# A fused attention and mixer kernel: the first channel product of the last two token groups as seven half products instead of eight

## Chip, cores and metric

The kernel runs on one core of one Trainium2 chip. The metric is the device time of one execution in microseconds (us). The engines are PE (TensorE; PEld is its weight load), DVE (VectorE), ACT (ScalarE), POOL (GpSimd) and SP (SyncE, which here only issues DMAs). Differences under about 0.5% (4.15 us here) can't be told from no change by a measurement of this kernel.

## What is computed

With 8 batches, 8 heads, 576 tokens and head size 64, and with d_model 512, 256 token-mixing and 1536 channel-mixing units:

```python
q_s = softmax(q, axis=-1);  k_s = softmax(k, axis=2)           # over features, over tokens
x   = q_s @ (k_s^T @ v)                                        # per head, put together to (8, 576, 512)
xt  = x.transpose(0, 2, 1)
u   = x + (relu(xt @ w_tok1) @ w_tok2).transpose(0, 2, 1)      # token mixing
out = u + relu(u @ w_ch1) @ w_ch2                              # channel mixing: "ch1", then "ch2"
```

## The kernel before

**Tiling.** The 8 x 576 tokens are cut into nine groups of 512 tokens. A group's u is kept transposed, channels on the partitions, as four tiles of 128 channels x 512 tokens (index n), each split into a high and a low float32r part (`uh`, `ul`). There are three such slots, which the groups take in turn (`uT`, L355). ch1 is cut into twelve row blocks f of 128 hidden channels; the weights of block f stand in `cw[f]` as four parts: 0 and 1 are ch1's high and low part, 2 and 3 ch2's.

**A step** is one (group, f). `ch1(g, f)` (L400) runs 12 matmuls of 512 columns: for each n, low weights by high tokens, high by high, high by low. ACT takes the relu into `h2h` (L410) and DVE the rounding rest into `h2l` (L411). `ch2` (L415) adds 12 more matmuls into four accumulators `ps_o`, one for each n of the output. In the main loop (L564) ch1 of a step is written ahead of ch2 of the step before it, so that the relu has a whole ch1 to finish in. After a group's last step `residual` (L427) adds `uh` and `ul` on POOL into `stg` tiles (a pool of two buffers of 128 x 1024 floats), and `out_end` (L436) adds the accumulators on DVE into these `stg` tiles and sends them out.

**Attention beside it.** The 32 units (batch, head pair) of attention and token mixing are spread over the steps up to the group before the last but one, one unit every three steps (`put`, L544; `todo`). A unit uses all engines: `softmax_k` subtracts a maximum on POOL (`k_t`, L235); `softmax_q` ends in a split of q whose rest is made on POOL (`ql`, L115); `stage_qT` turns q on DVE and copies 32 x 32 blocks back in 16 pieces (L321, eleven on DVE, five on ACT), which must wait for `ql`, since they write over its input; `stage_h1` and `stage_u` make the token mixing: the relu `hh` on ACT (L350), its rest `hl` on DVE (L351), and matmuls that take both (L379).

**What sets the order.** The program is written as above, but a scheduler of the build reorders the instructions of each engine; the order is then fixed, and each engine runs its own list strictly in turn. Loads are issued by SP in such a list too: `q_t`, `v_t`, `k_t` and `kt_t` for the units.

## Time and profile before

| | |
|---|---|
| runs | 827.21, 830.62, 830.99 us; median 830.62 |
| the profiled execution | 830.2 us, of which 828.3 us are the span of the profile |
| TensorE clock granted | 1.00 in the whole span |
| PE / PEld busy | 796.6 us (96%) / 669.5 us (81%) |
| DVE / ACT / POOL busy | 487.7 us (59%) / 331.6 us (40%) / 113.0 us (14%) |
| ch1, L407 | 1296 matmuls of 128 x 512; ch2, L419: as many |
| DMA | 63.54 MB, 77 GB/s on average |

Rows of the time line give start, duration, engine, source line, operation, out<-in, count, and in brackets the idle time ahead with what ended it. Rows of groups end in busy time, mean duration in ns and idle time. Rows of waits give total us, how often, the longest. Matmuls are pipelined: the distance of their starts is their cost, not the duration in the row (390 ns for 512 columns).

### The profile page before, as it was taken

To read this page: it belongs to the slowest core of one execution; us is meant where nothing else is said; L and a number is where in the kernel's file an instruction comes from. 1 tells how busy PE (TensorE), PEld (TensorE's weight loads), DVE (VectorE), ACT (ScalarE), POOL (GpSimd) and SP (SyncE) were. 2 spreads that over 40 slices of the span, in tenths; PEclk is the share of its full clock that TensorE was granted. 3 is DMA by queue.
4 is the path that set the end of the run, shared out by engine and by line. 5 is a ranking of instruction groups with operands and counts; after the bars stand their busy time and mean duration, and the time that the engine had idled before them with its cause. 6 is when DMAs were issued, how large, how long until landed. Compare 5 with 4: busy or idle time off the path is not lost.

```text
span 828.3 us, 11791 instructions
## 1 busy us (share of the span) xinstructions
PE 796.6 (96%) x4464; PEld 669.5 (81%) x4464; DVE 487.7 (59%) x1084; ACT 331.6 (40%) x822; POOL 113.0 (14%) x93
## 2 busy tenths in 40 slices
PE   4799999988999999999999999999999999999997
PEld 3688888777888888788888888888888888888886
DVE  6899998899775555665556554755566322112112
ACT  6876534455543344344434443344434321011110
POOL 1000000112220111311113111311131102001000
PEclk9999999999999999999999999999999999999999
DMA  9753433423212122322232211321131001001001
GB/s 297 235 160 94 146 108 102 138 76 114 90 48 92 53 63 60 100 63 63 63 113 63 63 47 36 108 63 53 42 97 47 15 1 51 1 0 51 1 1 51
DMA packets 60632, 63.54 MB, mean 77 GB/s; under 512 B 40864, under 2 KB 40992, under 8 KB 60576
## 3 DMA queue, kind: packets, MB, share of 16 engines
q1 hardware_dynamic: 55392, 53.36, 21.9%
q10 hardware_dynamic: 5184, 9.44, 3.0%
q8 instruction: 35, 0.57, 0.3%
q14 instruction: 21, 0.17, 0.1%
HBM read 53.35 MB, written 9.44 MB: 76 GB/s over the span
## 4 chain that ended last, share of the span: by engine, by line
PE 77%; DVE 11%; DMA 6%; issue 2%; ACT 2%; POOL 1%; SPq 1%; DVEq 0%; POOLq 0%; ACTq 0%
PE ps_h L407 30%; PE ps_o L419 30%; PE ps_h L379 6%; PE ps_h L335 5%; DVE q_t L321 3%; DMA out<-stg 2%; PE ps_h L275 2%; DMA q_t<-in_q 2%; PE ps_h L343 1%; PE ps_o L379 1%; DMA stg<-in_w 1%; PE ps_h L233 1%; DVE st L243 1%; POOL ql L115 1%; DMA kt_t<-in_kt 1%
## 5 line engine op out<-in xcount | busy, mean ns | idle before, releaser
L407 PE MATMUL ps_h<-uh,cw 128*128 128x512 f32 x864 | 268.3, 391 | 1.3 <-DVE cw L115 1.3
L419 PE MATMUL ps_o<-h2h,cw 128*128 128x512 f32 x864 | 250.0, 391 | 0.0
L419 PEld LDWEIGHTS ps_o<-h2h,cw 128*128 128x128 f32 x864 | 160.2, 188 | 32.6 <-ACT h2h L410 0.2
L407 PEld LDWEIGHTS ps_h<-uh,cw 128*128 128x128 f32 x864 | 159.3, 188 | 32.4 <-DVE cw L115 1.7
L411 DVE SCALAR_TENSOR_TENSOR h2l<-ps_h,h2h 128x512 fp32r<-128x512 f32 x108 | 74.3, 688 | 171.3 <-ACT h2h L410 170.2
L407 PE MATMUL ps_h<-ul,cw 128*128 128x512 f32 x432 | 168.6, 390 | 0.0
L410 ACT ACTIVATE h2h<-ps_h 128x512 fp32r<-128x512 f32 x108 | 64.6, 598 | 251.0 <-PE ps_h L407 234.6
L419 PE MATMUL ps_o<-h2l,cw 128*128 128x512 f32 x432 | 151.9, 395 | 1.0 <-DVE h2l L411 1.0
L321 DVE COPY q_t<-cv_s 32x160 f32<-32x160 f32 (+1 forms) x264 | 70.5, 267 | 63.9 <-POOL ql L115 60.6
L407 PEld LDWEIGHTS ps_h<-ul,cw 128*128 128x128 f32 x432 | 81.1, 188 | 17.4
L419 PEld LDWEIGHTS ps_o<-h2l,cw 128*128 128x128 f32 x432 | 79.6, 188 | 17.4 <-DVE h2l L411 1.4
L235 POOL TENSOR_TENSOR k_t<-k_t,mb 128x640 f32<-128x640 f32 x24 | 38.1, 1586 | 298.6 <-ACT mb L234 298.6
L115 POOL TENSOR_TENSOR ql<-q_t,qh 128x640 fp32r<-128x640 f32 x24 | 37.6, 1566 | 211.9 <-ACT qh L114 180.8
L432 POOL TENSOR_TENSOR stg<-uh,ul 128x512 f32<-128x512 f32 x28 | 35.6, 1292 | 143.5 <-DMA out<-stg 118.8
L243 DVE TENSOR_REDUCE st<-q_t 128x10 f32<-128x640 f32 x32 | 26.2, 818 | 37.6 <-DMA q_t<-in_q 37.5
L254 ACT ACTIVATE q_t<-q_t 128x640 f32<-128x640 f32 x28 | 20.7, 741 | 44.3 <-DVE q_t L253 40.8
L321 ACT COPY q_t<-cv_s 32x128 f32<-32x128 f32 (+1 forms) x120 | 36.8, 307 | 1.9 <-DVE cv_s L313 0.5
L379 PE MATMUL ps_h<-w2h,hl 128*128 128x320 f32 (+1 forms) x112 | 30.1, 302 | 4.3 <-DVE hl L351 4.1
L379 PE MATMUL ps_h<-w2h,hh 128*128 128x256 f32 (+1 forms) x112 | 32.7, 299 | 0.0
L379 PE MATMUL ps_h<-w2l,hh 128*128 128x256 f32 (+1 forms) x112 | 32.6, 296 | 0.0
L386 ACT CAST uh<-ps_h 128x320 fp32r<-128x320 f32 (+4 forms) x76 | 24.5, 339 | 14.7 <-PE ps_h L379 9.0
L387 DVE TENSOR_TENSOR ul<-ps_h,uh 128x320 fp32r<-128x320 f32 (+4 forms) x76 | 26.7, 372 | 5.3 <-ACT uh L386 4.4
(140 smaller groups left out, 1048.4 us busy)
## 6 DMA issues: line engine op xcount, KB each, us to landing
stg<-in_w SPq DMA_DIRECT2D x28, 512.0 KB, 4.1
kt_t<-in_kt SPq DMA_DIRECT2D x32, 320.0 KB, 3.5
q_t<-in_q SPq DMA_DIRECT2D x32, 320.0 KB, 3.0
v_t<-in_v SPq DMA_DIRECT2D x64, 128.0 KB, 3.1
out<-stg ACTq DMA_DIRECT2D x32, 256.0 KB, 3.2
k_t<-in_k SPq DMA_DIRECT2D x24, 320.0 KB, 3.6
v_t<-in_v SPq DMA_DIRECT2D x32, 32.0 KB, 3.2
out<-part ACTq DMA_DIRECT2D x4, 256.0 KB, 2.6
```

What stands on the lines that cost most here:

```text
L115: lo_eng.tensor_tensor(lo, src, f32(hi), op=ALU.subtract)
L235: nc.gpsimd.tensor_tensor(kx, kx, mb.unsqueeze(1).broadcast_to([P, C1, P]), op=ALU.subtract)
L243: nc.vector.tensor_reduce(st[:, 0, :], qt, axis=AX.X, op=ALU.max)
L321: eng(qx[ys, 0:n, xs], turned[xs, 0:n, ys])
L335: nc.tensor.matmul(y[:, 0:TOK], a, w, start=(i == 0), stop=(i == len(mm) - 1))
L379: nc.tensor.matmul(t[:, 0:N], a, w, start=(i == 0), stop=(i == len(mm) - 1))
L387: nc.vector.tensor_tensor(ul, src, f32(uh), op=ALU.subtract).ins,
L407: nc.tensor.matmul(t, cw[f][x][:, n, :], w, start=(i == 0), stop=(i == 3 * NJ - 1))
L410: nc.scalar.activation(hh, t, AF.Relu).ins,
L411: nc.vector.scalar_tensor_tensor(hl, t, 0.0, f32(hh), op0=ALU.max, op1=ALU.subtract).ins,
L419: nc.tensor.matmul(o, cw[f][x][:, n, :], w, start=(first and i == 0), stop=(last and i == 2))
L432: nc.gpsimd.tensor_tensor(res[n], f32(uh), f32(ul), op=ALU.add)
```

## The change

For the last two groups (but for the first two row blocks of the last group but one) two row blocks fa, fb are taken together as a pair. Their ch1 is seen as a 2 x 2 block product: two row blocks by two halves of the contraction (n = 0, 1 and n = 2, 3), times two halves of the contraction by two halves of the tokens (256 each). Eight half products of 6 matmuls with 256 columns would be what stands there now; the new `pair` makes seven, four of them with sums of weight blocks and four with sums of token blocks, and puts the results together by adds on DVE before the relu. There are eleven such pairs: five of the last group but one, six of the last.

- `weight_sums(p)` makes the four sums of the weights of pair p, splits them and writes high and low part to a buffer in memory: on POOL two adds of 128 x 512, four of 128 x 256 and one subtraction of 128 x 1024, on ACT one copy of 128 x 1024, on SP two DMAs of 512 KB in rows of 512 B. It takes two tiles of the `stg` pool. The six calls are put two to a group into the fourth, fifth and sixth group, whose other work is the attention units.
- `load_sum` brings the sums back, 256 KB for each half product in two DMAs, to five places in `cw` that are free by then; each is started when the place's last user is done, five half products ahead.
- `token_sums(g)` makes four sums of token blocks on DVE (nine operations of 128 x 512) and splits them (four copies on ACT, four subtractions on DVE).
- In `pair` each half product goes through one or two adds on DVE (128 x 256; the first is copied by ACT), and the relu and its rest are made in four pieces of 128 x 256 instead of two of 128 x 512. ch2 of the pair before is written between the half products (`between`).

```diff
+    HC = CW // 2
+    def weight_sums(p):
+        a, b = cw[2 * p], cw[2 * p + 1]
+        x = stg.tile([P, CW, 2], U32, name="stg").rearrange("p n w -> p (n w)")
+        xf, xr = x.bitcast(F32), x.bitcast(F32R)
+        for i, (hi, lo) in enumerate((a[:2], b[:2])):
+            both = xf[:, i * CW : (i + 1) * CW].rearrange("p (n m) -> p n m", n=NJ)
+            nc.gpsimd.tensor_tensor(both, f32(hi), f32(lo), op=ALU.add)
+        a11, a12, a21, a22 = (xf[:, i * HC : (i + 1) * HC] for i in range(4))
+        nc.gpsimd.tensor_tensor(a22, a21, a22, op=ALU.add)
+        nc.gpsimd.tensor_tensor(a21, a11, a21, op=ALU.subtract)
+        nc.gpsimd.tensor_tensor(a11, a22, a11, op=ALU.subtract)
+        nc.gpsimd.tensor_tensor(a12, a12, a11, op=ALU.subtract)
+        h = stg.tile([P, CW, 2], U32, name="stg").rearrange("p n w -> p (n w)").bitcast(F32R)
+        nc.scalar.copy(h, xf)
+        nc.gpsimd.tensor_tensor(xr, xf, f32(h), op=ALU.subtract)
+        for i, t in enumerate((h, xr)):
+            src = f32(t).rearrange("p (k n m) -> p k n m", k=4, n=2)
+            nc.sync.dma_start(sums[p][:, :, :, i, :], src)
...
+    def token_sums(g, place, tmp):
...
+        def cut(k, t):
+            hi, lo = place[k]
+            split(hi, lo, t, nc.vector)
...
+    def product(weights, rows):
+        t = ps_h.tile([P, 512], F32, name="ps_h")[:, 0:HC]
+        i = 0
+        for n in range(2):
+            uh, ul = (x[:, n, :] for x in rows)
+            for x, w in ((1, uh), (0, uh), (0, ul)):
+                nc.tensor.matmul(t, weights(x, n), w, start=(i == 0), stop=(i == 5))
+                i += 1
+        return t
...
+        def drain(f, t, src):
+            hh, hl = (x[:, t * HC : (t + 1) * HC] for x in hs[f])
+            nc.scalar.activation(hh, src, AF.Relu)
+            nc.vector.scalar_tensor_tensor(hl, src, 0.0, f32(hh), op0=ALU.max, op1=ALU.subtract)
...
+        nc.scalar.copy(v0, product(own(fa, 0), half(0, 0)))
+        plus(v1, own_sum(S2, tsum[g, 2]), v0)
+        between(0)
+        plus(v0, product(own(fa, 2), half(1, 0)), v0)
+        drain(0, 0, v0)
+        plus(v2, own_sum(S3, tsum[g, 3]), v1)
+        between(1)
+        t = own_sum(S1, tsum[g, 1])
+        plus(v3, t, v2)
+        plus(v1, t, v1)
+        drain(1, 1, v3)
+        plus(v2, product(own(fb, 2), tsum[g, 4]), v2)
+        drain(1, 0, v2)
+        between(2)
+        plus(v1, own_sum(S4, half(1, 1)), v1)
+        drain(0, 1, v1)
+        between(3)
...
+    for p in range(NF // 2):
+        put(n0 + NF * (p // 2 + 1) + (5, 9)[p % 2], lambda p=p: weight_sums(p))
```

**What moves on POOL.** The first place is POOL's list at the start of the fourth group, the first of the three groups that take weight sums. Before it reads as follows (`k_t` and `ql` belong to the units, `stg<-uh,ul` is `residual` of the group that begins).

```order
L235 TENSOR_TENSOR k_t<-k_t,mb 128x640
L432 TENSOR_TENSOR stg<-uh_101,ul_105 128x512 x2
L115 TENSOR_TENSOR ql<-q_t,qh 128x640
L432 TENSOR_TENSOR stg<-uh_101,ul_105 128x512 x2
L235 TENSOR_TENSOR k_t<-k_t,mb 128x640
L115 TENSOR_TENSOR ql<-q_t,qh 128x640
```

Now the list begins at the same `k_t` so (L443 to L451 are `weight_sums`; the other lines stand one further down, `residual` is L570):

```order
L236 TENSOR_TENSOR k_t<-k_t,mb 128x640
L443 TENSOR_TENSOR stg<-cw_117 128x512 x2
L116 TENSOR_TENSOR ql<-q_t,qh 128x640
L445 TENSOR_TENSOR stg<-stg 128x256
L446 TENSOR_TENSOR stg<-stg 128x256
L447 TENSOR_TENSOR stg<-stg 128x256
L448 TENSOR_TENSOR stg<-stg 128x256
L451 TENSOR_TENSOR stg<-stg 128x1024
L443 TENSOR_TENSOR stg<-cw_117 128x512 x2
```

After the four small adds of the second sums, the same list goes on to the next unit:

```order
L448 TENSOR_TENSOR stg<-stg 128x256
L236 TENSOR_TENSOR k_t<-k_t,mb 128x640
L451 TENSOR_TENSOR stg<-stg 128x1024
L570 TENSOR_TENSOR stg<-uh_101,ul_105 128x512 x2
L116 TENSOR_TENSOR ql<-q_t,qh 128x640
L570 TENSOR_TENSOR stg<-uh_101,ul_105 128x512 x2
```

So the first sums stand where `residual` stood, around the first unit's `ql`, and `residual` has moved one unit later, around the second `ql`, behind the second sums. The same change stands at the start of the fifth and sixth group. The order of PE's list is the same as before up to the first pair.

**What moves on ACT** at the same place: the copy of the first sums (L450) has come in between the relu `hh` of the unit and the relu of a step.

```order
L351 ACTIVATE hh<-ps_h 128x256
L450 CAST stg<-stg 128x1024
L411 ACTIVATE h2h_108<-ps_h 128x512
L115 CAST qth<-q_t 128x576
L387 CAST uh_100<-ps_h 128x256
```

Without the row of L450 these are the rows of before. What POOL subtracts in L451 waits for it.

**What moves on DVE** where the pairs begin, at the end of the last unit and the change from the seventh to the eighth group. Before:

```order
L387 TENSOR_TENSOR ul_104<-ps_h,uh_100 128x64
L387 TENSOR_TENSOR ul_106<-ps_h,uh_102 128x320
L387 TENSOR_TENSOR ul_106<-ps_h,uh_102 128x192
L443 TENSOR_TENSOR stg<-ps_o,stg 128x512 x4
L411 SCALAR_TENSOR_TENSOR h2l_112<-ps_h,h2h_108 128x512
L411 SCALAR_TENSOR_TENSOR h2l_113<-ps_h,h2h_109 128x512
```

Now, from the fifth token sum behind the last `ul` on (L466 and L116 are `token_sums`, `tmp` its intermediate sums, L581 is `out_end`):

```order
L466 TENSOR_TENSOR tmp_6670<-tmp_6670,ul_106 128x512
L581 TENSOR_TENSOR stg<-ps_o,stg 128x512
L466 TENSOR_TENSOR tmp_6672<-tmp_6672,ul_104 128x512
L581 TENSOR_TENSOR stg<-ps_o,stg 128x512
L466 TENSOR_TENSOR tmp_6673<-tmp_6673,ul_104 128x512
L581 TENSOR_TENSOR stg<-ps_o,stg 128x512
L466 TENSOR_TENSOR tmp_6670<-tmp_6670,ul_106 128x512
L581 TENSOR_TENSOR stg<-ps_o,stg 128x512
L412 SCALAR_TENSOR_TENSOR h2l_112<-ps_h,h2h_108 128x512
L116 TENSOR_TENSOR ul_105<-tmp_6672,uh_101 128x512
L116 TENSOR_TENSOR ul_105<-tmp_6673,uh_101 128x512
L412 SCALAR_TENSOR_TENSOR h2l_113<-ps_h,h2h_109 128x512
```

The token sums of both groups have been drawn forward between the adds of `out_end` and the rests of the two single steps; those of the last group go on into the first pair, where ten more operations of 128 x 512 stand between the pair's own eleven of 128 x 256.

## The prediction, made before the changed kernel was run

> **What bounds the kernel now.** I read the page's busy shares and its chain first, then the waits of PE from the third group on, then the time lines of the stretches that the change touches.

> ```profile
> PE 796.6 (96%) x4464; PEld 669.5 (81%) x4464; DVE 487.7 (59%) x1084; ACT 331.6 (40%) x822; POOL 113.0 (14%) x93
> ...
> PE 77%; DVE 11%; DMA 6%; issue 2%; ACT 2%; POOL 1%; SPq 1%; DVEq 0%; POOLq 0%; ACTq 0%
> ```
> ```profile
> PE ps_h L379 <- DVE hl L351: 2.7, 3, 1.7
> ```

> PE is the bound, and behind 250 us it is almost never late: three waits with 2.7 us in all, each where a unit's matmuls L379 need `hl`. So matmuls saved are time saved, and any new wait of PE is time lost. The busy shares say nothing of the second; the stretches do.

> **Part 1, the matmuls.** The cost of a matmul is the distance of starts. One stretch of PE's time line has both widths:

> ```profile
> 336.33 0.62 PE L407 MATMUL ps_h<-uh,cw 128*128 128x512 f32 x2
> ...
> 339.05 0.28 PE L335 MATMUL ps_h<-w1h,qh 128*128 128x256 f32 x1
> ...
> 340.72 0.64 PE L419 MATMUL ps_o<-h2h,cw 128*128 128x512 f32 x2
> ...
> ```

> From 336.33 to 339.05 run 12 matmuls of 512 columns: 2.72 us, 0.2267 each. From 339.05 to 340.72 run the 14 of L335 with 256 columns, each with its own weights: 1.67 us, 0.1193 each, 5% above the half. A pair had 24 x 0.2267 = 5.44 us of ch1 and gets 42 x 0.1193 = 5.01; it saves 0.43 us instead of the 0.68 of an exact eighth. Eleven pairs: **-4.7 us**. That is the whole gain; ch2 is unchanged.

> **Part 2, the weight sums in groups four to six.** They are off PE, but their POOL work stands ahead of things that PE waits for. Start of the fourth group, POOL, DVE and ACT:

> ```profile
> 335.70 1.57 POOL L235 TENSOR_TENSOR k_t<-k_t,mb 128x640 f32<-128x640 f32 x1 [15.28 <-ACT mb L234]
> 343.17 2.53 POOL L432 TENSOR_TENSOR stg<-uh,ul 128x512 f32<-128x512 f32 x2 [5.89 <-DMA out<-stg]
> 345.66 1.56 POOL L115 TENSOR_TENSOR ql<-q_t,qh 128x640 fp32r<-128x640 f32 x1
> 347.18 2.54 POOL L432 TENSOR_TENSOR stg<-uh,ul 128x512 f32<-128x512 f32 x2
> 359.65 1.57 POOL L235 TENSOR_TENSOR k_t<-k_t,mb 128x640 f32<-128x640 f32 x1 [9.93 <-ACT mb L234]
> 365.81 1.57 POOL L115 TENSOR_TENSOR ql<-q_t,qh 128x640 fp32r<-128x640 f32 x1 [4.60 <-ACT qh L114]
> ```
> ```profile
> 347.26 4.79 DVE L321 COPY q_t<-cv_s 32x160 f32<-32x160 f32 x11 [4.57 <-POOL ql L115]
> 352.08 0.42 DVE L351 SCALAR_TENSOR_TENSOR hl<-ps_h,hh 128x256 fp32r<-128x256 f32 x1
> ...
> 367.42 2.73 DVE L321 COPY q_t<-cv_s 32x160 f32<-32x160 f32 x11 [2.81 <-POOL ql L115]
> ```
> ```profile
> 340.93 0.73 ACT L114 CAST qh<-q_t 128x640 fp32r<-128x640 f32 x1 [0.58 <-PE ps_h L335]
> ...
> 349.17 0.39 ACT L350 ACTIVATE hh<-ps_h 128x256 fp32r<-128x256 f32 x1
> ...
> 352.44 0.68 ACT L114 CAST qth<-q_t 128x576 fp32r<-128x576 f32 x1 [1.87 <-DVE q_t L321]
> ...
> 358.68 0.74 ACT L254 ACTIVATE q_t<-q_t 128x640 f32<-128x640 f32 x1 [1.42 <-DVE q_t L253]
> ```
> ```profile
> 352.56 0.38 PE L379 MATMUL ps_h<-w2h,hl 128*128 128x256 f32 x1 [1.67 <-DVE hl L351]
> ...
> 374.77 0.28 PE L379 MATMUL ps_h<-w2h,hl 128*128 128x256 f32 x1
> ```

> The eleven copies take 2.73 us alone and 4.79 us where two adds of POOL (2.54 us) run beside them: while POOL works, a copy gets on at a fifth of its pace (0.48 us of work in 2.54). That made `hl` late and is the 1.67 us wait of PE at 352.56.

> [...]

> POOL's prices: 1.27 us for 512 elements, 1.57 for 640, so 0.30 for each 128; an add of 256 is 0.67 and a subtraction of 1024 is 2.47. ACT: 0.73 for 640, 0.68 for 576; a copy of 1024 is 1.03.

> *First sums of a group.* The adds of 512 take the time that `residual` had, `ql` comes as before at 347.2. Then four small adds, 2.7 us, to 349.9; ACT, free since 349.56, copies to 350.95; POOL subtracts to 353.4. The copies on DVE get through 0.2 x 2.7 = 0.5 us of their 2.73 by 349.9, 1.05 more by 350.95, and meet the long subtraction with 1.2 us left: another 0.5 beside it, the rest by 354.1. Before they ended at 352.05. PE already waits there, so all of it shows: **+2.0 us** a group. The cause is narrow: with 1.2 us less left there is no meeting and `hl` is as early as before. Bounds: -0.3 (POOL's second half of `residual` is gone from there) and +2.5 (the whole subtraction).

> *Second sums.* They stand ahead of the next `ql`, and so does `residual`. Their tile is free when POOL has done the first subtraction and the first of the DMAs has landed.

> ```profile
> stg<-in_w SPq DMA_DIRECT2D x28, 512.0 KB, 4.1
> ...
> out<-stg ACTq DMA_DIRECT2D x32, 256.0 KB, 3.2
> ```

> The nearest row to a DMA of 512 KB is the load of as much, 4.1 us; the store of half as much took 3.2. With 4.1: landed at 355.05, two adds and four small ones to 360.3; `k_t` at its own time moved by PE's 2.0, 361.65 to 363.2; ACT's copy (behind the exponential, 361.4) to 362.45; the subtraction to 365.7; the copy's DMA landed at 366.55; first half of `residual` to 369.1, `ql` to 370.65 (367.4 + 2.0 = 369.4 on the old plan). The copies again run beside the second half of `residual`: 4.79 us, then `hl`, 375.9. PE needs `hl` at 374.77 + 2.0 = 376.8. The margin of 0.9 covers it; but it is gone if either DMA lands 1 us later, so I take **+0.5 us** a group, bounds 0 and 3. SP issues these stores between `kt_t` and the next `q_t`, which went out at 353.97 only; queued behind a store, `q_t` may land 1 us later, inside the same margin.

> ```profile
> 353.97 0.33 SPq L140 DMA_DIRECT2D q_t<-in_q  x1
> ```

> Three groups: 3 x 2.5 = **+7.5 us**, bounds -0.9 and 16.5.

> **Part 3, where the pairs begin.** DVE, PE and POOL at the change to the eighth group:

> ```profile
> 689.55 0.23 DVE L387 TENSOR_TENSOR ul<-ps_h,uh 128x64 fp32r<-128x64 f32 x1 [1.05 <-ACT uh L386]
> 690.35 0.76 DVE L387 TENSOR_TENSOR ul<-ps_h,uh 128x320 fp32r<-128x320 f32 x2 [0.57 <-ACT uh L386]
> 692.64 2.05 DVE L443 TENSOR_TENSOR stg<-ps_o,stg 128x512 f32<-128x512 f32 x3 [1.53 <-PE ps_o L419]
> ...
> 695.96 0.68 DVE L411 SCALAR_TENSOR_TENSOR h2l<-ps_h,h2h 128x512 fp32r<-128x512 f32 x1
> ```
> ```profile
> 697.88 0.62 PE L407 MATMUL ps_h<-uh,cw 128*128 128x512 f32 x2
> ```
> ```profile
> 696.26 5.03 POOL L432 TENSOR_TENSOR stg<-uh,ul 128x512 f32<-128x512 f32 x4 [36.92 <-DMA out<-stg]
> ```

> An operation of 512 on DVE is 0.68 us, one of 256 is 0.42. From 689.8 on (behind the `ul` of 64) the list holds two token sums, 0.76 of `ul`, eight more sums or cuts and four adds of `out_end`: 14 x 0.68 + 0.76 = 10.3, to 700.1; the first single step's rest ends at 700.8 instead of 696.6, the second's, behind two cuts, at 702.9. PE has finished ch1 of the second step at 697.88 and goes on with 18 half matmuls and 8 of ch2 until it needs the first rest, 3.96 us: 701.8. That just holds. Then the first pair: the second half product of pair two needs the PSUM buffer of the fifth before it. PE would start it 48 half and 24 full matmuls behind 697.88, at 709.05; DVE frees the buffer behind eight operations of 512 and six of 256 from 702.9, at 710.85: 1.8 us late, and 0.4 more at the next buffer. **+2.2 us**, bounds 0 and 6.

> Later pairs have 11 x 0.42 = 4.6 us of DVE in 5.01 + 5.44 us of PE; each half product has four PSUM buffers. The last pair's relu (add 0.42, relu 0.39, rest 0.42) lies beside six matmuls of ch2, 1.36 us, and two more before the rest is needed: nothing. `load_sum` starts five half products, some 7 us, ahead of use; its 128 KB pieces are like the stores above, 3.2 us: nothing.

> **The sum**, against the profiled execution's 830.2 us (0.4 below the median of the runs): 830.2 - 4.7 + 7.5 + 2.2 = **835.2 us**. By its bounds alone it goes from 824.6 to 848.

> **Rivals.**

> *The meeting does not take place* (ends not slower). If between POOL's small adds, each of which waits for the one before, DVE slips in a second copy each time, the copies are through before 350.95. Then part 2 is 3 x 0.5 and the time is 830.2 - 4.7 + 1.5 + 2.2 = 829.2; with part 3 hidden too, 827. For it: the margin is 1 us or so. Against: POOL's adds before followed each other without a gap that let copies through.

> *The memory buffer chain is late.* The second `ql` hangs on two DMAs in a row, and with 1.8 us more for each (5.9, of which the loads of 512 KB stayed below at the median) the second `hl` is 2.7 us late in each group: 835.2 + 3 x 2.2 = 842; with a longer delay 848. For it: rows of 512 B are smaller than any store's here. Against: the DMA engines are idle for three quarters of that stretch (share 0.23 in the row of windows, whose last columns are clock, DMA share and GB/s).

> ```profile
> 354.00:376.00 22.00, 22.00 (x131) 18.76 (x130) 12.06 (x29) 9.14 (x22) 3.13 (x2) 1.00 0.23 59
> ```

> *POOL blocks DVE's token sums.* In the changed list `residual` of the eighth group (four adds, 5.03 us) runs when `out_end` has gone out, about 702 to 707, beside the token sums. If each of its adds holds up an operation as it holds up a copy, DVE loses four fifths of 5.03 us, 4.0, in front of the pair's buffers: 835.2 + 3.5 = 838.7. No row here has such an operation wholly beside POOL, so it stays a rival with a small chance.

> [...]

> *Half matmuls do not keep their distance*, because a weight load of 189 ns would bound them: 11 x (42 x 0.189 - 5.44) = +27.5 against today's ch1, 830.2 + 27.5 + 9.7 = 867 us. The 0.1193 of L335, with a new load for every matmul, speaks against it.

> ```profile
> L335 PEld LDWEIGHTS ps_h<-w1h,qh 128*128 128x128 f32 x96 | 18.1, 189 | 0.9
> ```

> **Numbers.** Forecast 0.43 (own range 832.5 to 838), no meeting 0.32 (826 to 831), late buffers 0.12, blocked token sums 0.11, weight loads 0.02. The range 826.8 to 845.5 leaves out the last rival and the ends of the others. Faster by over 0.5% (below 826.5; 0.5% is about what a measurement of this kernel can tell from no change) needs the whole of the gain and no wait at all: 0.10. Within 0.5% (to 834.8) lie the rest of "no meeting" and the lower part of the forecast: 0.42. Slower: 0.48.

> **What would show it.** Right: 0.119 us between half matmuls of L494; at the start of groups four to six the first eleven copies (L322) last about 6.8 us with a long POOL subtraction (L451) over their end, and PE waits there some 3.7 us for `hl` instead of 1.67; 2 us of PE waits for PSUM buffers in the first pairs; none later. Wrong: copies at or below 4.8 us there (the meeting failed), PE waits at the second unit of those groups above 1 us (the DMAs), waits of PE inside the later pairs, or a distance of half matmuls other than 0.119.

## The result, and the profile after

The changed kernel takes 840.62 us (median of four runs, 840.0 to 842.13), the kernel before beside it 830.38 (827.21 to 830.99): a ratio of 1.0134, 95% interval 1.0105 to 1.0163. The forecast was 835.2, slower by 0.6%; the time lies inside the range (826.8 to 845.5), but the loss is twice the one forecast. The profiled execution took 840.67 us, with a span of 838.9.

The page after, its busy shares and the engines' shares of the chain:

```profile
PE 800.4 (95%) x4662; PEld 680.9 (81%) x4662; DVE 560.7 (67%) x1209; ACT 351.3 (42%) x869; POOL 163.4 (19%) x135
...
PE 70%; DVE 16%; DMA 5%; issue 4%; ACT 2%; POOL 2%; SPq 1%; DVEq 0%; ACTq 0%; POOLq 0%
```

PE went from 77% of the chain to 70%, DVE from 11% to 16%: PE now waits for DVE. The waits of PE behind 250 us say where (total, how often, longest):

```profile
PE ps_h L380 <- DVE hl L352: 11.7, 6, 4.0
PE ps_h L494 <- DVE mix L533: 1.8, 1, 1.8
```

Before it was 2.7 us in three waits. The six are the first and second units of groups four to six, and the one below stands in the second pair. POOL, DVE and PE at the start of the fourth group:

```profile
349.70 2.37 POOL L451 TENSOR_TENSOR stg<-stg 128x1024 fp32r<-128x1024 f32 x1 [1.16 <-ACT stg L450]
...
369.60 2.52 POOL L570 TENSOR_TENSOR stg<-uh,ul 128x512 f32<-128x512 f32 x2 [3.44 <-issue]
372.08 1.55 POOL L116 TENSOR_TENSOR ql<-q_t,qh 128x640 fp32r<-128x640 f32 x1
373.59 2.54 POOL L570 TENSOR_TENSOR stg<-uh,ul 128x512 f32<-128x512 f32 x2
```
```profile
345.44 6.96 DVE L322 COPY q_t<-cv_s 32x160 f32<-32x160 f32 x11 [4.75 <-POOL ql L116]
352.42 0.42 DVE L352 SCALAR_TENSOR_TENSOR hl<-ps_h,hh 128x256 fp32r<-128x256 f32 x1
...
373.67 4.80 DVE L322 COPY q_t<-cv_s 32x160 f32<-32x160 f32 x11 [4.83 <-POOL ql L116]
```
```profile
352.90 0.58 PE L380 MATMUL ps_h<-w2h,hl 128*128 128x256 f32 x1 [4.02 <-DVE hl L352]
...
354.99 1.05 PE L408 MATMUL ps_h<-uh,cw 128*128 128x512 f32 x2
355.85 0.63 PE L408 MATMUL ps_h<-ul,cw 128*128 128x512 f32 x1
356.27 1.05 PE L408 MATMUL ps_h<-uh,cw 128*128 128x512 f32 x2
...
358.62 0.62 PE L408 MATMUL ps_h<-uh,cw 128*128 128x512 f32 x2
359.08 0.39 PE L408 MATMUL ps_h<-ul,cw 128*128 128x512 f32 x1
```

The meeting took place as forecast: the eleven copies last 6.96 us (forecast 6.8) with the long subtraction L451 over their end, and PE waits 4.02 (forecast 3.7). But look at the matmuls behind the wait: from 354.99 to 356.27 three of 512 columns take 1.28 us, 0.43 each; from 358.62 to 359.08 two take 0.46, 0.23 each. The windows of that place show why. Columns: length, busy time of PE, PEld, DVE, ACT, POOL, then the TensorE clock, DMA share, GB/s.

```profile
348.10:351.51 3.41, 0.78 (x6) 0.52 (x4) 3.33 (x7) 1.54 (x2) 2.25 (x2) 1.00 0.17 52
351.51:354.92 3.41, 2.02 (x8) 2.02 (x9) 3.37 (x5) 1.04 (x2) 2.16 (x3) 0.50 0.82 237
354.92:358.34 3.42, 3.42 (x10) 2.71 (x9) 1.52 (x4) 0.43 (x1) 3.18 (x4) 0.50 0.36 114
358.34:361.75 3.41, 3.41 (x33) 2.65 (x32) 1.91 (x4) 0.78 (x3) 1.20 (x2) 1.00 0.00 0
```

The granted clock falls to 0.50 for exactly two stretches of 3.41 us, the first of which begins while PE is still waiting. PE is busy for 2.02 + 3.42 us of them at half pace: 2.7 us lost on top of the wait. The same happens behind the waits at 541.80 and 723.16, for one stretch each (1.7 us lost at each). The last, with the stretch ahead of it:

```profile
720.15:723.56 3.41, 1.58 (x12) 1.22 (x11) 3.41 (x8) 1.71 (x4) 0.00 (x0) 1.00 0.36 105
723.56:726.98 3.42, 3.42 (x18) 3.42 (x18) 3.21 (x9) 0.86 (x3) 0.00 (x0) 0.50 0.29 77
```

The profile's account of the 10.6 us that the span grew:

| | forecast | in the trace after |
|---|---|---|
| matmuls of the pairs | -4.7 | -4.9 (two versions without waits, below) |
| waits at first and second units | +7.5 | +9.0 (11.7 - 2.7) |
| wait where the pairs begin | +2.2 | +1.8 |
| half clock behind waits | not priced | +6.1 (2.7 + 1.7 + 1.7) |
| start of the kernel, up to the fourth group | 0 | -2.25 |

The last row is the first add of `out_end` of the third group, at 336.19 in the trace before and at 333.94 after. The change does not reach there; runs below with the same work up to that place differ by as much (the same 14 `v_t,k_t` matmuls start at 334.17 with the weight sums alone and at 332.25 with the same sums without stores). So this row is luck. The rows make 9.75; the brackets count a wait from the modelled end of the last matmul, some 0.15 us late each (a row of 512 columns lasts 0.39 us where the starts lie 0.23 apart), which is most of the rest.

### The profile page after: what moved, and what is told of

The parts are those of the page before. It is cut to its first block, busy times and chain, and to the rows that moved or that the text cites. A ratio compares the mean times of both kernels' runs of the same rounds, so it can differ in the third digit from the quotient of the medians.

```text
span 838.9 us, 12691 instructions
## 1 busy us (share of the span) xinstructions
PE 800.4 (95%) x4662; PEld 680.9 (81%) x4662; DVE 560.7 (67%) x1209; ACT 351.3 (42%) x869; POOL 163.4 (19%) x135
## 4 chain that ended last, share of the span: by engine, by line
PE 70%; DVE 16%; DMA 5%; issue 4%; ACT 2%; POOL 2%; SPq 1%; DVEq 0%; ACTq 0%; POOLq 0%
PE ps_o L421 26%; PE ps_h L408 21%; PE ps_h L380 6%; PE ps_h L494 6%; DVE q_t L322 6%; PE ps_h L336 4%; PE ps_h L276 2%; DMA out<-stg 2%; PE ps_o L380 1%; POOL ql L116 1%; DVE stg L581 1%; DVE tmp L466 1%; PE ps_h L344 1%; DMA stg<-in_w 1%; PE ps_h L234 1%
## 5 line engine op out<-in xcount | busy, mean ns | idle before, releaser
L421 PE MATMUL ps_o<-h2h,cw 128*128 128x512 f32 x768 | 221.2, 392 | 0.0
L408 PE MATMUL ps_h<-uh,cw 128*128 128x512 f32 x688 | 216.0, 395 | 1.1 <-DVE cw L116 1.1
L421 PEld LDWEIGHTS ps_o<-h2h,cw 128*128 128x128 f32 x768 | 140.7, 188 | 27.2 <-ACT h2h L411 0.2
L408 PE MATMUL ps_h<-ul,cw 128*128 128x512 f32 x344 | 135.4, 394 | 0.0
L421 PE MATMUL ps_o<-h2l,cw 128*128 128x512 f32 x384 | 133.2, 395 | 1.0 <-DVE h2l L412 1.0
L322 DVE COPY q_t<-cv_s 32x160 f32<-32x160 f32 (+1 forms) x264 | 83.2, 315 | 67.8 <-POOL ql L116 64.5
L411 ACT ACTIVATE h2h<-ps_h 128x512 fp32r<-128x512 f32 x86 | 51.3, 597 | 131.7 <-PE ps_h L408 122.1
L412 DVE SCALAR_TENSOR_TENSOR h2l<-ps_h,h2h 128x512 fp32r<-128x512 f32 x86 | 58.8, 684 | 60.4 <-ACT h2h L411 59.2
L408 PEld LDWEIGHTS ps_h<-ul,cw 128*128 128x128 f32 x344 | 65.3, 190 | 14.3
L116 POOL TENSOR_TENSOR ql<-q_t,qh 128x640 fp32r<-128x640 f32 x24 | 37.6, 1565 | 195.9 <-ACT qh L115 174.8
L570 POOL TENSOR_TENSOR stg<-uh,ul 128x512 f32<-128x512 f32 x28 | 37.2, 1349 | 138.7 <-DVE h2l L530 59.9
L533 DVE TENSOR_TENSOR mix<-ps_h,mix 128x256 f32<-128x256 f32 x77 | 31.2, 422 | 45.6 <-PE ps_h L494 45.3
L494 PE MATMUL ps_h<-uh,cw 128*128 128x256 f32 x212 | 41.2, 289 | 1.8 <-DVE mix L533 1.8
L494 PEld LDWEIGHTS ps_h<-uh,cw 128*128 128x128 f32 x212 | 36.1, 197 | 4.8 <-DVE mix L533 2.2
L322 ACT COPY q_t<-cv_s 32x128 f32<-32x128 f32 (+1 forms) x120 | 36.8, 307 | 1.9 <-DVE cv_s L314 0.5
## 6 DMA issues: line engine op xcount, KB each, us to landing
stg<-in_w SPq DMA_DIRECT2D x28, 512.0 KB, 3.9
out<-stg ACTq DMA_DIRECT2D x32, 256.0 KB, 3.4
sums<-stg SPq DMA_DIRECT2D x12, 512.0 KB, 3.6
```

Source lines behind the costliest of these rows:

```text
L116: lo_eng.tensor_tensor(lo, src, f32(hi), op=ALU.subtract)
L322: eng(qx[ys, 0:n, xs], turned[xs, 0:n, ys])
L408: nc.tensor.matmul(t, cw[f][x][:, n, :], w, start=(i == 0), stop=(i == 3 * NJ - 1))
L411: nc.scalar.activation(hh, t, AF.Relu).ins,
L412: nc.vector.scalar_tensor_tensor(hl, t, 0.0, f32(hh), op0=ALU.max, op1=ALU.subtract).ins,
L421: nc.tensor.matmul(o, a, w, start=(first and i == 0), stop=(last and i == len(mm) - 1))
```

## Experiments

The theory that the trace after suggests (A in the expectations): the loss is PE's waits beside the weight sums and at the first pairs, and the half clock behind them, while the pairs gain what their matmul distances say. The rival (B): the half products, their adds and the streamed weights lose the time themselves. All ratios are to the kernel before on the same chip, whose medians were 828.2 to 830.7 us.

**The pairs alone**, `weight_sums` and `load_sum` left out:

```diff
-    for p in range(NF // 2):
-        put(n0 + NF * (p // 2 + 1) + (5, 9)[p % 2], lambda p=p: weight_sums(p))
...
-        if i < len(queue):
+        if False:
```

> The pairs and the token sums alone: no weight sums are made, stored or brought back, and the own weights of a block stand in the place of the sums, so the outputs of the last two groups are not the reference's. Theory A (the loss lies in PE's waits at the units that stand beside the weight sums, in the wait at the start of the pairs, and in the half TensorE clock behind such waits; the pairs themselves gain 5.0 us): waits at the unit starts as in the kernel before (about 1.8, 0.6, 0.75 us), clock 1.00 there, one wait of about 2 us at the first pairs with up to 1.7 us of half clock behind it: 830.4 - 5.0 + 2.0 + 0 to 1.7 = 827.4 to 829.1 us. Theory B (the half products or their adds lose the time): about 840 us.

827.09 us, ratio 0.9988 (0.9979 to 0.9998). The waits of PE behind 250 us:

```profile
PE ps_h L380 <- DVE hl L352: 2.3, 3, 1.1
PE ps_h L492 <- DVE mix L531: 1.8, 1, 1.8
```

The unit waits are those of the kernel before, the wait in the second pair is there, with one stretch of half clock behind it (0.50 from 709.46 to 712.88). B falls for the pairs and their adds. The streamed weights are left out here; the last version below has them.

**The weight sums alone**, put into the kernel before and never used:

```diff
+    for p in range(NF // 2):
+        put(n0 + NF * (p // 2 + 1) + (5, 9)[p % 2], lambda p=p: weight_sums(p))
```

> The kernel before with the weight sums made and stored, but never used: all of ch1 as before. Theory A: PE waits of 4.0, 2.3 and 2.9 us at the first units of groups four to six and of 0.8 to 1.4 at the second ones, 9.5 us more than before, and one or two clock windows of 3.4 us at half speed behind the longest, 1.7 us each: 830.4 + 9.5 + 1.7 to 5.1 = 841.6 to 845 us. Theory B: 830 to 832 us, as the sums are off the path.

845.61 us, ratio 1.0206 (1.0185 to 1.0227): sums that nobody reads cost more than the whole change.

```profile
PE ps_h L379 <- DVE hl L351: 12.8, 6, 3.6
```

The three waits at the first units (3.6, 2.8 and 3.0 us) each have one stretch of half clock behind them (mean granted clock of the span 0.990; 1.000 in the trace before). The span grew by 15.2 us against the trace before: 10.1 us of waits and 5.1 of half clock, as A said in kind. The median lies just above A's 845 us.

**The same without the stores:**

```diff
-        for i, t in enumerate((h, xr)):
-            src = f32(t).rearrange("p (k n m) -> p k n m", k=4, n=2)
-            nc.sync.dma_start(sums[p][:, :, :, i, :], src)
```

> As the kernel before with the weight sums, but without the two stores of each: the sums stay in the two tiles and are overwritten. Theory A says that the first waits of a group come from the long subtraction on POOL over the eleven copies: they stay at 4.0, 2.3 and 2.9 us, with the clock windows behind them; and that the second waits come from the landing of the stores, without which the first half of residual and the next ql come 3 us earlier: below 0.3 us at the second units. 830.4 + 6.3 + 1.7 to 5.1 = 838.4 to 841.8 us. Theory C (the second waits come from the length of POOL's work alone): they stay at 0.8 to 1.4 us and the time is that of the run with the stores, 841.6 to 845.

845.7 us, ratio 1.0212 (1.0197 to 1.0227). Half of it came as A said: at the second units no wait is left, so those come from the stores. Without them `residual` has both its tiles at once, runs in one piece ahead of `ql`, and the second copies are free (2.73 us instead of 4.80). The other half missed: the first waits did not stay. They are 3.5, 4.0 and 4.1 us, so they grew in the fifth and sixth group. POOL and DVE in the fourth group:

```profile
348.11 2.39 POOL L439 TENSOR_TENSOR stg<-stg 128x1024 fp32r<-128x1024 f32 x1 [1.16 <-ACT stg L438]
350.58 2.49 POOL L431 TENSOR_TENSOR stg<-cw 128x512 f32<-128x512 f32 x2
```
```profile
343.83 8.09 DVE L321 COPY q_t<-cv_s 32x160 f32<-32x160 f32 x11 [3.08 <-POOL ql L115]
...
373.35 2.73 DVE L321 COPY q_t<-cv_s 32x160 f32<-32x160 f32 x11 [4.99 <-POOL ql L115]
```
```profile
PE ps_h L379 <- DVE hl L351: 11.8, 4, 4.1
```

With no store to wait for, POOL goes straight from the subtraction to the next sums, and the copies meet these too: 8.09 us. In the fourth group `ql` also came earlier, so the wait there is no longer than with the stores. Two stretches of half clock stand behind each of the three first waits, six in all (mean granted clock of the span 0.984, with the stores 0.990). So the 3.5 us saved at the second units were lost again, 2.3 us in longer first waits and some 3 us in half clock, an estimate from three more stretches of 1.7 us each, less what PE waits in them; a start that was 1.9 us earlier in this execution makes up most of the rest.

**The long subtraction behind the unit's `hl`**, in the version without stores. A POOL operation of one element reads `hl`, and L446 (L439 above) is ordered behind it. The first sums are also written some steps earlier in the program; what comes in POOL's list at this place, and in which order, is otherwise the same:

```diff
+        return [nc.gpsimd.tensor_tensor(seen, f32(u["hl"][:, 0, 0:1]), f32(u["qtl"][:, 0:1]), op=ALU.add).ins]
...
-        nc.gpsimd.tensor_tensor(xr, xf, f32(h), op=ALU.subtract)
+        with behind(gate()):
+            nc.gpsimd.tensor_tensor(xr, xf, f32(h), op=ALU.subtract)
```

> The kernel before with the weight sums and without stores, as in the run without stores, but in the first sums of a group the long subtraction on POOL stands behind the unit's hl, so it can't lie over the eleven copies; POOL does the same work. Theory A (the meeting of the copies with the long subtraction makes the first waits): each eleven copies that took about 7 us take some 5, the first waits fall by about 1.7 us each, from 3.7, 4.1 and 4.3 to 2.0 to 2.6, the clock loses at most one window of 3.4 us in the groups instead of six, second waits 0 to 1 us: 834 to 838 us. Rival (POOL's amount of work, whatever it lies beside, makes them): first waits of 3.7 to 4.3 us and 845 us as without the change.

834.72 us, ratio 1.0077 (1.0054 to 1.01). POOL, DVE and the waits of PE:

```profile
351.12 0.19 POOL L428 TENSOR_TENSOR seen<-hl,qtl 128x1 f32<-128x1 f32 x1 [2.34 <-DVE hl L351]
351.26 2.41 POOL L446 TENSOR_TENSOR stg<-stg 128x1024 fp32r<-128x1024 f32 x1
```
```profile
345.68 4.90 DVE L321 COPY q_t<-cv_s 32x160 f32<-32x160 f32 x11 [3.46 <-POOL ql L115]
```
```profile
PE ps_h L379 <- ACT hh L350: 3.4, 3, 1.2
PE ps_h L379 <- DVE hl L351: 3.0, 4, 0.9
```

Same work on POOL, 11 us less: the copies take 4.90 us instead of 8.09, the first waits are below 1 us, and the clock stays at 1.00 behind 250 us (mean of the whole span 0.996 instead of 0.984). That shows the meeting as the cause of the first waits. What is left at the second units (1.2 us each) is now ACT's `hh`, behind its own share of the copies, late by the late `ql`.

**The last group's token sums later**, in the changed kernel:

```diff
-            token_sums(g, {k + 1: row[2 * k : 2 * k + 2] for k in range(4)}, tmp)
+            with behind(lastop):
+                token_sums(g, {k + 1: row[2 * k : 2 * k + 2] for k in range(4)}, tmp)
```

`lastop` is the pair's last rest L530 on DVE.

> The changed kernel, with only the token sums of the last group moved: they stand behind the second pair's last operation on DVE and no longer among the first pair's adds. Theory A1 (the wait of 2.0 us at the first pairs comes from these thirteen operations of 512 in front of the adds that free a PSUM buffer): the wait is below 0.3 us, the clock stays at 1.00 there, 840.6 - 2.0 - 1.7 = 836.9 us. Theory A2 (it comes from the residual on POOL, which stretches four of the first token sums' operations by 3.2 us in all): the wait stays at 1 to 2 us, 838.5 to 840.6.

839.89 us, ratio 1.014 (1.0111 to 1.0168), the changed kernel's own. The wait in the second pair is gone, and with it the half clock there (mean granted clock of the span 0.992, in the changed kernel 0.990):

```profile
PE ps_h L380 <- DVE hl L352: 14.2, 7, 3.7
```

From the same 16 `v_t,k_t` matmuls of PE in the seventh group (at 621.42 here, at 617.39 in the changed kernel) to the end it took 218.0 us instead of 221.5; A1 had named 2.0 + 1.7. But in this execution the waits at the units were 2.5 us longer, with three stretches of half clock, so the time shows nothing of it. It does not decide between A1 and A2: `residual` came later here and lay over one of the token sums' operations only.

**Residual gated in the kernel before**, to see what POOL's order alone is worth. `residual` of groups three to seven stands behind the third unit's `hl`:

```diff
-        if last and g > 1:
+        if last and g > NG - 3:
             residual(g)
...
+    for g in range(2, NG - 2):
+        n = (g + 1) * NJ + 2
+        put(n0 + (g - 2) * NF + 3 * 2 + 1.5, lambda n=n, g=g: residual(g, passed(units[n])))
```

> The kernel before, with residual of groups three to seven behind the third unit's hl and nothing else changed, to tell what of a better version is due to the order of POOL alone. Theory A: the three waits of 1.8, 0.6 and 0.75 us go, 830.4 - 3.2 = 827.2 us, and a changed kernel that is ordered so stays some 5 us below this one. Rival (the waits come from the copies' own length or from ql): they stay and the time is 830 us.

824.24 us, ratio 0.9956 (0.9941 to 0.9971): no wait of PE is left behind 250 us, and 3.9 us are gone beside a kernel before of 828.17, where A had 3.2.

**Everything gated in the changed kernel:** one weight sum to each of groups three to seven, its adds, its subtraction and `residual` behind the `hl` of three units in turn; the sum for the first pair and `residual` of the eighth group behind that group's first pair; the token sums as above.

```diff
+    for g in range(2, NG - 2):
+        at_unit(g, 0, lambda gate, p=g - 1: sum_adds(p, gate))
+        at_unit(g, 1, lambda gate, p=g - 1: sum_rest(p, gate))
+        at_unit(g, 2, lambda gate, g=g: residual(g, gate))
```

> The changed kernel with the same work in other places. Each of groups three to seven takes one weight sum (the sum of the first pair, which only the last group needs, comes behind the first pair of the eighth group); its adds stand behind the first unit's hl on POOL, its long subtraction behind the second unit's, residual behind the third's, each held by a POOL operation of one element that reads hl; the last group's token sums stand behind the second pair. Theory A: no copy has POOL beside it, so the waits at the units go, those of the kernel before too, the wait at the pairs goes, the clock stays at 1.00 from 250 us on, and the gain of the pairs is all that is left beside the kernel before with residual gated alone (824.2 us): 824.2 - 5.0 = 819.2 us, or 818 to 822. Rival (the sums cost PE wherever they stand, through SP's queue, memory or k_t held up behind the gates): waits of 1 to 3 us a group at other places, 824 to 834 us.

821.09 us, ratio 0.9891 (0.9867 to 0.9916). The same sums now cost nothing at the units. One wait is left, in the pairs. POOL, DVE and PE's waits there:

```profile
713.64 6.92 POOL L588 TENSOR_TENSOR stg<-uh,ul 128x512 f32<-128x512 f32 x4 [1.79 <-issue]
```
```profile
713.63 0.69 DVE L481 TENSOR_TENSOR tmp<-uh 128x512 f32<-128x512 f32 x1
714.35 1.67 DVE L481 TENSOR_TENSOR tmp<-tmp,ul 128x512 f32<-128x512 f32 x1
```
```profile
PE ps_h L509 <- DVE mix L550: 1.1, 1, 1.1
```

A token sum beside `residual` takes 1.67 us, the first one, which begins with it, 0.69.

**The token sums one pair later still**, behind the third pair, out of the way of `residual`:

```diff
-        if i == 1:
+        if i == 2:
             g = NG - 1
```

> As the run with all sums gated, with the last group's token sums one pair later, behind the third pair's last operation on DVE, so that residual of the eighth group on POOL no longer lies beside them. There four of their operations took 1.4 to 1.8 us instead of 0.68, and PE waited 1.3 us for a PSUM buffer behind them. If POOL's stretching of two-input operations on DVE makes that wait, it goes, nothing is late from 250 us to the end, and the time is 821.1 - 1.3 = 819.8 us. Rival (the thirteen operations are too many for one pair, whatever lies beside them): a wait of 1 to 2 us comes back one pair later and the time stays at 821 us.

819.53 us, ratio 0.9888 (0.9864 to 0.9911). The thirteen operations stand in one pair as before, and nothing waits: PE is busy without a break in the window from 250 to 800 us, at a clock of 1.00.

```profile
250.00:800.00 550.00, 550.00 (x3245) 472.47 (x3244) 306.13 (x714) 208.40 (x497) 148.19 (x123) 1.00 0.30 84
```

So at this place it was POOL that made the wait, not the number of operations. The trace shows this, the time does not: the ratio is that of the version above. Beside it, in the same rounds, the gated kernel before:

> The kernel before with residual gated, once more, on the same chip and in the same rounds as the best version of the changed kernel, so that the pairs' own worth can be read without any wait on either side. If the eleven pairs are worth what their matmul distances say, this one is 5 us slower than the other; if the half products, their adds or the streamed sums cost something off the waits, less.

824.39 us, ratio 0.9942 (0.992 to 0.9963). With no wait on either side behind 250 us the pairs, streamed weights included, are worth 824.39 - 819.53 = 4.9 us.

**The clock by itself.** A first probe delayed the rest `h2l` in the kernel before by dummy operations on DVE.

> The kernel before, with 8, 9, 10, 11, 12 and 13 operations of 128 x 512 on DVE put ahead of the rest h2l of the second, fifth and eighth step of the last two groups, so that PE, undisturbed by anything else, waits there for about 0.4, 1.0, 1.6, 2.2, 2.8 and 3.4 us (0.60 us an operation, against a slack of 3.9). Theory A (an idle PE costs the clock): behind the waits of 2.2 us and more the granted clock is 0.50 for whole windows of 3.4 us that lie on one grid, matmuls of 512 columns start 0.42 us apart there instead of 0.23, and the time is 830.4 + 11 + 3 to 5 us of clock = 845 to 847. Rival (the half clock seen in the changed kernel has another cause, such as the weight sums): the clock stays at 1.00 and the time is 830.4 + 11 = 841.

830.73 us: it tells nothing, since the build's scheduler moved other matmuls ahead and PE never waited there. The second probe makes a delay that no order gets around, in the gated kernel before:

```diff
+    turns = {(7, 2): 10, (7, 5): 12, (7, 8): 13, (8, 2): 14, (8, 5): 16, (8, 8): 20}
...
+        for _ in range(turns.get((g, f), 0)):
+            x = uT[g][0][:, 0, :]
+            nc.vector.tensor_tensor(x, f32(x), f32(x), op=ALU.max)
```

> The kernel before with residual gated, which has no wait of PE behind 250 us, and in it 10, 12, 13 in the eighth and 14, 16 and 20 operations on DVE in the ninth group that write the group's first token tile onto itself (the larger of x and x), so that the next step's matmuls must wait for the last of them, in whatever order PE has them. From (n + 2) x 0.60 us against 7.4 us of other work, PE should wait some 0, 1.3, 1.9, 2.5, 3.7 and 6.1 us, 15.5 in all. Theory A (an idle PE costs the clock): no change of clock behind the first two, windows of 3.4 us at half clock behind the last two and perhaps behind the 1.9 and 2.5, starting on one grid, 1.5 us each: 824.2 + 15.5 + 3 to 8 = 843 to 848 us. Rival (the half clock has to do with the weight sums' work on POOL and memory, not with the wait): the clock stays at 1.00, 840 us.

835.98 us, a single run, below both forecasts. The waits of PE are shorter than I had worked out, 8.9 us in all instead of 15.5:

```profile
PE ps_h L409 <- DVE uh L413: 8.9, 4, 5.3
```

They are 0.2, 1.0, 2.38 and 5.29 us. Only behind the last does the clock fall; the stretches around the third and the fourth, on the grid that the fall shows:

```profile
783.50:786.91 3.41, 2.64 (x12) 1.87 (x10) 3.27 (x5) 0.00 (x0) 0.00 (x0) 1.00 0.00 0
786.91:790.33 3.42, 1.80 (x8) 1.48 (x9) 1.50 (x3) 0.00 (x0) 0.00 (x0) 1.00 0.00 0
...
803.98:807.39 3.41, 1.20 (x6) 0.66 (x4) 3.27 (x5) 0.00 (x0) 0.00 (x0) 1.00 0.00 0
807.39:810.80 3.41, 0.33 (x1) 0.33 (x2) 2.90 (x5) 0.00 (x0) 0.30 (x1) 0.50 0.00 0
810.80:814.22 3.42, 3.42 (x9) 2.65 (x9) 0.00 (x0) 0.00 (x0) 3.42 (x3) 0.50 0.02 5
```

The wait of 2.38 us is split over two stretches that keep PE busy for 2.64 and 1.80 us, and the clock stays; a stretch with 1.20 us busy is followed by one at half clock. There are no weight sums in this kernel: the half clock comes from the idle PE, and the rival falls. The two stretches at 0.50, with PE busy for 0.33 + 3.42 us, cost 1.9 us; 824.2 + 8.9 + 1.9 makes 835.0 of the 835.98.

## Why the prediction was wrong

It took the right side for mostly the right reasons, and half the size. By its steps:

*Part 1, the matmuls: right.* Nine half matmuls from 709.70 to 710.77 are 0.119 us each, as taken from L335.

```profile
709.70 0.40 PE L494 MATMUL ps_h<-uh,cw 128*128 128x256 f32 x2
...
710.77 0.63 PE L421 MATMUL ps_o<-h2h,cw 128*128 128x512 f32 x2
```

The gain was put at 4.7 us; it is 4.9 between the two versions without waits, whose runs each spread over some 2 us.

*Part 2, first sums: right.* Copies of 6.8 us were forecast and are 6.96; the three first waits grew by 6.3 us in all, from 2.7 to 9.0 (6.0 forecast). The run with the subtraction behind `hl` shows the cause. The rival "the meeting does not take place" is out.

*Part 2, second sums: the mechanism that I called covered was not.* I took 0.5 us a group, with the remark that the margin of 0.9 goes if a DMA lands 1 us later. These waits are 1.4, 0.8 and 1.0 us by the distance of starts: 3.2 in all instead of 1.5. The version without stores has none, so they hang on the stores. SP's row of the second sums' two stores, and the page's row of all stores (KB each, median us from issue to landing):

```profile
364.93 1.78 SPq L454 DMA_DIRECT2D sums<-stg  x2
```
```profile
sums<-stg SPq DMA_DIRECT2D x12, 512.0 KB, 3.6
```

At the median a store lands 3.6 us behind its issue (4.1 taken). But in the fourth group the second sums' first store went out at 364.93, behind a `kt_t` load in SP's list and 1.2 us after ACT's copy had ended, and landed 4.6 us later, just before `residual` began (369.60). So the chain over memory was late, as in the rival of late buffers, but by less than its 2.7 us a group, and in part because of a late issue.

*Part 3: right in size.* Forecast 2.2 us, measured 1.8, at the second half product of the second pair, as said. Its working was less good. I kept POOL's stretching of the token sums as a rival, yet it happened:

```profile
710.55 6.40 POOL L570 TENSOR_TENSOR stg<-uh,ul 128x512 f32<-128x512 f32 x4 [39.39 <-DMA out<-stg]
```
```profile
703.45 0.68 DVE L466 TENSOR_TENSOR tmp<-uh 128x512 f32<-128x512 f32 x1
...
710.66 0.68 DVE L412 SCALAR_TENSOR_TENSOR h2l<-ps_h,h2h 128x512 fp32r<-128x512 f32 x1
711.26 2.84 DVE L116 TENSOR_TENSOR ul<-tmp,uh 128x512 fp32r<-128x512 f32 x2
714.02 0.68 DVE L412 SCALAR_TENSOR_TENSOR h2l<-ps_h,h2h 128x512 fp32r<-128x512 f32 x1
714.62 1.17 DVE L466 TENSOR_TENSOR tmp<-uh,tmp 128x512 f32<-128x512 f32 x1
715.72 1.78 DVE L116 TENSOR_TENSOR sumh<-tmp,sumh 128x512 fp32r<-128x512 f32 x1
```

Four operations took 5.8 us instead of 2.7, some 3 us that the forecast had left out. The other error has the other sign. I priced an operation of 512 on DVE by its duration in the row, 0.68 us, but in an unbroken run the starts lie 0.60 us apart: twelve from 703.45 to 710.66. The rows of 256 overlap likewise (717.42, 0.41 us long, and the next at 717.75). Over the 26 operations of 512 and six of 256 that I counted this makes 2.5 us too much. So the size came out right by two errors, which is luck. The four operations that took 1.14 to 1.78 us beside `residual`, instead of 0.68, have both inputs in SBUF; the rest L412 at 714.02, which reads PSUM, took its 0.68 us there.

*The sum: the step that failed.* It added the waits at a granted clock of 1.00, as the table of before had it for the whole span, and priced nothing for what a wait does to the matmuls behind it. That is 6.1 us in the profiled execution, more than half of the loss of 10.2 us and more than the 5.2 us by which the forecast fell short. The second units add 1.7; the early start of the profiled execution (2.25 us) hides about as much, by luck. PE's waits in the kernel before (1.67 us at most behind 250 us, at a clock of 1.00) never brought it up, and the forecast's own waits of 3.7 us lay outside what the trace of before could show.

## What to carry to other kernels

In these runs a new wait of PE cost more than its length where it left PE idle for about half of a clock stretch of 3.41 us (1.58 us busy brought half clock, 1.80 did not): 1.7 us more for each full stretch at half clock. Several short waits were cheaper than one long one: in the run with the subtraction held back, seven waits of at most 1.2 us, 6.4 in all, left the clock at 1.00 behind 250 us. Work on POOL that nobody waits for still needs a place. Beside it the eleven copies L322 took 6.96 us here instead of 2.73 alone, and a token sum's operation with both inputs in SBUF up to 1.78 instead of 0.68: look in the trace for what DVE does beside it, put it where it stretches nothing, and hold it there with an operation of one element that reads what must be done first. Put into good order, this change is worth its 4.9 us, and the same rule is worth 3.9 us in the kernel without it (828.17 to 824.24).

## What the runs showed of the hardware

```profile
363.80 2.39 DVE L257 TENSOR_SCALAR st<-st 128x10 f32<-128x10 f32 x1
```
